# First block in 2 KB rows, wide warm-up matmuls, mask bias by one matmul per bank, first weight part gated one load sooner

## Chip, cores and metric

The kernel runs on one core of one Trainium2 chip. The time is in device microseconds for one launch; lower is better. The median of 9 runs before the change is 224.55 us (223.74 to 226.69).

## The reference, cut to what matters

Sliding-window attention with sinks, for 4 batches of 8 heads, 768 tokens and head size 64, followed by a two-layer feed-forward block on the concatenated heads. A query sees the keys of the last 128 tokens (itself included) and the first 4 tokens of its sequence.

```python
scores = (1 / sqrt(64)) * q @ k.T                      # (4, 8, 768, 768)
keep = (key < 4) | ((0 <= query - key) & (query - key < 128))
a = softmax(where(keep, scores, -1e9))
x = (a @ v).transpose(0, 2, 1, 3).reshape(3072, 512)   # heads side by side
h = x @ w_in                                           # (3072, 2048)
out = (h * sigmoid(1.702 * h)) @ w_out                 # (3072, 512), float32
```

All inputs and the output are float32; the kernel computes in float16 with float32 sums.

## The kernel before, in words

The 3072 tokens are cut into 12 blocks of 256 (`TB`), three to a batch. Each block goes through the same stages: its q, k and v are loaded and cast to float16; q and k are turned so that the head dimension lies on the partitions; scores are computed for four pairs of heads; ACT takes their exponentials; the probabilities are multiplied by v and normalised on DVE; the result x is turned; then x is multiplied by w_in (`mm1`, 64 matmuls of 256 columns), ACT and DVE apply the gate, and the result is multiplied by w_out (`mm2`, 32 matmuls of 512 columns). mm1 of block k stands beside the attention of block k+1, and mm2 of block k beside that of block k+2.

**The order is planned.** Every piece of work is an `Op` with an engine (or several to choose from), an estimated duration, its dependencies, and a due time `prio`. `Plan.run` lays the operations out in time by these estimates, choosing at each step the ready operation that can start first, and by due time among those within 20 ns. It also hands out PSUM banks. Each engine then runs its list strictly in that order on the chip, whatever the real durations are. A change to an estimate, a size or a due time can therefore change the order of work on every engine. Wherever the plan leaves TensorE idle in its first 12 us, `run` puts in filler matmuls on zeros (L142 to L146, `warm` at L883).

**Loads.** `load(k)` issues q, k and v of a block. Block 0 (L409 to L417) comes in eight pieces of 128 KB, four of q on the SyncE queue and four of k on the ACT queue, each with rows of 1 KB; blocks 1 to 3 (L418 to L425) come as two pieces for q and two for k, with rows of 2 KB; later ones in one piece each. q and k of block 1 and v of blocks 0 and 1 are on the SyncE queue, behind q of block 0. The constants, the weights and block 2 are issued by GpSimd (POOL); the weights come in eight parts, w0 to w3 of w_in and w4 to w7 of w_out, cast to float16 by the DMA. A load issued by SyncE or ACT also waits until the one eight before it has landed, since eight semaphores take turns. Some loads are gated by hand (L861 to L879): w0 waits for the last of the four loads of block 1 (`o_first[-1]`).

**Turning and scores of block 0.** The four quarters of block 0 are cast one by one (`o_cqk`), and `turn_two_pairs` turns two pairs of heads of q or k with four TensorE transposes and two copies. So the pairs 0 and 1 can be turned, and their scores computed, when the first half of block 0 is in. Blocks 1 to 3 use `turn_on_pe`, which needs both halves of q (or of k), since each holds every second head; it transposes for every head pair at once, for even or odd token groups. From block 4 on the DMA transposes.

**Mask.** For blocks 0 and 1 the mask is added into the PSUM bank of the scores ahead of them: per bank, three or four matmuls of 128 columns put a bias tile (0 or -60000) there, with the bias as stationary operand and the identity as moving one (L633 to L639). Later blocks multiply the exponentials by a 0/1 mask on DVE (L675).

**Casts.** Casts of blocks 0 and 1 go to DVE, ACT or POOL by the plan's choice; later ones go to POOL. Copies of any kind show as line L282, the helper `copy`; they are told apart by the tiles: qk and v for casts, blkT for copies of turned q and k.

## Time and profile before

| | |
|---|---|
| median of 9 runs | 224.55 us |
| profiled execution: time, span | 223.8 us, 222.0 us |
| TensorE (PE) busy | 215.6 us, 97% of the span |
| DVE / ACT / POOL busy | 127.2 / 125.3 / 86.0 us |
| mm1 matmuls (L775), 768 | 98.7 us, 273 ns each |
| mm2 matmuls (L804), 400 | 99.0 us, 371 ns each |
| filler matmuls (L884), 97 | 7.7 us |
| moved by DMA | 36.42 MB, mean 164 GB/s |

In the rows of the timeline the first number is the start in us from the span's beginning, the second the duration, then engine, line, operation, output and inputs, the count, and in brackets the idle time of the engine before it with what ended the wait. Engine names with a q are the queues that issue transfers, not the transfers. Matmuls overlap, so a row of eight can last a little longer than the distance to the next one; the chain of waits gives those distances. Rows of the windows give, after the stretch and its length, the busy time of PE, PEld, DVE, ACT and POOL with their instruction counts, the granted TensorE clock, the DMA share and the GB/s.

### The profile page before, as it was taken

The page shows a single profiled execution, that of the slowest core. Times are in us where ns is not written, and L with a number is a line of the kernel's source. Part 1 is how long each engine was busy: PE and PEld are TensorE (multiplying, and loading weights), DVE is VectorE, ACT ScalarE, POOL GpSimd, SP SyncE. Part 2 cuts the span into 40 slices and gives each one's busy share as a digit, 9 for nine tenths or more (in the row PEclk, how much of TensorE's full clock was granted, in tenths as well). Part 3 has the DMA queues.
Part 4 walks back from the last instruction along what each step waited for, and adds up shares of the span by engine and source line. Part 5 has one row for each costly group of instructions (what it writes and reads, how often), then busy time and mean ns, then how long its engine had stood idle before and what let it go on. Part 6 is the DMA issues. An engine that isn't in the chain of part 4 may idle for free.

```text
span 222.0 us, 5454 instructions
## 1 busy us (share of the span) xinstructions
PE 215.6 (97%) x2184; PEld 151.1 (68%) x2184; DVE 127.2 (57%) x281; ACT 125.3 (56%) x244; POOL 86.0 (39%) x145
## 2 busy tenths in 40 slices
PE   8989999999999999999999999999999999999993
PEld 8767987467856766766666666767667666666652
DVE  3679766267854865665655664676465655634310
ACT  3676655666747675566476475555476476444320
POOL 3069422665993685801923937507500000000000
PEclk9999999999999999999999999999999999999999
DMA  5999999997948979379399589399442212221223
GB/s 169 301 216 200 191 300 216 326 293 225 270 107 177 274 153 295 76 150 283 94 205 264 78 196 255 69 216 241 93 99 49 64 34 47 52 68 24 50 47 95
DMA packets 66344, 36.42 MB, mean 164 GB/s; under 512 B 28016, under 2 KB 62064, under 8 KB 66320
## 3 DMA queue, kind: packets, MB, share of 16 engines
q1 hardware_dynamic: 60992, 30.06, 54.9%
q0 software_dynamic: 4592, 5.38, 13.1%
q10 hardware_dynamic: 736, 0.66, 1.0%
q8 instruction: 17, 0.28, 0.5%
q14 instruction: 7, 0.06, 0.1%
HBM read 27.43 MB, written 6.29 MB: 152 GB/s over the span
## 4 chain that ended last, share of the span: by engine, by line
PE 88%; DMA 6%; DVE 1%; ACT 1%; SPq 1%; issue 0%; ACTq 0%
PE bank L775 37%; PE bank L804 36%; PE bank L708 7%; PE bank L643 5%; DMA v<-in_v_dram 3%; DMA qk<-in_k_dram 2%; DMA out_dram<-osb 1%; PE bank L747 1%; PE bank L571 1%; PE bank L623 1%; PE bank L636 1%; DVE v L282 1%; ACT at L668 1%; SPq L421 1%; DVE at L675 0%
## 5 line engine op out<-in xcount | busy, mean ns | idle before, releaser
L804 PE MATMUL bank<-w_out,gT 128*128 128x512 f16 (+2 forms) x400 | 99.0, 371 | 0.0
L775 PE MATMUL bank<-xT,w_in 128*128 128x256 f16 x768 | 98.7, 273 | 0.0
L789 DVE SCALAR_TENSOR_TENSOR gT<-th,bank 128x512 f16<-128x512 f16 x96 | 65.5, 683 | 46.7 <-ACT th L787 45.8
L787 ACT ACTIVATE th<-bank 128x512 f16<-128x512 f32 x96 | 57.6, 602 | 57.0 <-PE bank L775 55.5
L775 PEld LDWEIGHTS <-w_in 128*128 128x128 f16 x768 | 73.2, 98 | 23.1 <-issue 1.6
L282 POOL CAST qk<-qk 64x512 f16<-64x512 f32 (+1 forms) x72 | 43.8, 612 | 43.3 <-DMA qk<-in_q_dram 34.9
L668 ACT ACTIVATE at<-bank 128x512 f16<-128x512 f32 (+1 forms) x96 | 48.9, 573 | 15.5 <-PE bank L643 14.3
L804 PEld LDWEIGHTS <-gT 128*128 128x128 f16 x400 | 36.2, 98 | 24.5 <-issue 1.4
L675 DVE TENSOR_TENSOR at<-at,bank 128x1024 f16<-128x1024 f16 (+1 forms) x40 | 25.7, 641 | 23.0 <-ACT at L668 23.0
L282 POOL CAST v<-v 64x512 f16<-64x512 f32 x42 | 26.3, 625 | 9.9 <-DMA v<-in_v_dram 8.0
L708 PE MATMUL bank<-v,at 128*128 128x65 f16 x352 | 21.4, 193 | 0.7 <-DVE v L282 0.5
L823 ACT ACTIVATE osb<-bank 128x512 f32<-128x512 f32 (+1 forms) x24 | 14.5, 602 | 12.4 <-PE bank L804 11.9
L708 PEld LDWEIGHTS <-at 128*128 128x128 f16 x352 | 17.6, 97 | 4.6 <-issue 0.7
L728 DVE TENSOR_TENSOR xb<-bank,rcp 128x256 f16<-128x256 f32 x36 | 15.1, 420 | 0.6
L708 PE MATMUL bank<-vs,ats 128*128 128x65 f16 x128 | 14.9, 193 | 0.0
L708 PEld LDWEIGHTS <-ats 128*128 128x128 f16 x128 | 11.9, 97 | 2.2 <-issue 0.2
L643 PE MATMUL bank<-blkT 64*128 64x256 f16 x192 | 13.5, 244 | 0.0
L643 PEld LDWEIGHTS <-blkT 64*128 64x128 f16 x256 | 8.1, 94 | 6.2 <-issue 3.8
L726 DVE RECIPROCAL rcp<-bank 128x4 f32<-128x4 f32 x48 | 8.5, 177 | 4.9 <-PE bank L708 4.2
L282 ACT COPY blkT<-bank 128x256 f16<-128x256 f16 (+1 forms) x17 | 6.7, 445 | 4.2 <-PE bank L571 2.1
L884 PE MATMUL bank<-zero 128*128 128x128 f16 x97 | 7.7, 244 | 1.0 <-DVE zero L296 1.0
L884 PEld LDWEIGHTS <-zero 128*128 128x128 f16 x97 | 6.9, 112 | 1.1 <-DVE zero L296 1.0
(46 smaller groups left out, 75.5 us busy)
## 6 DMA issues: line engine op xcount, KB each, us to landing
v<-in_v_dram SPq DMA_DIRECT2D x12, 512.0 KB, 7.0
out_dram<-osb SPq DMA_DIRECT2D x46, 128.0 KB, 3.7
qk<-in_q_dram SPq DMA_DIRECT2D x8, 512.0 KB, 4.4
qk<-in_k_dram SPq DMA_DIRECT2D x8, 512.0 KB, 5.8
w_in<-in_moe_w_in_dram POOLq DMA_DIRECT2D x4, 512.0 KB, 7.1
w_out<-in_moe_w_out_dram POOLq DMA_DIRECT2D x4, 512.0 KB, 12.2
qk<-in_q_dram SPq DMA_DIRECT2D x4, 256.0 KB, 5.6
qk<-in_k_dram SPq DMA_DIRECT2D x4, 256.0 KB, 5.7
```

The lines of the kernel that those rows point to most:

```text
L282: {"POOL": nc.gpsimd.tensor_copy, "DVE": nc.vector.tensor_copy, "ACT": nc.scalar.copy}[e](out=out, in_=in_)
L643: nc.tensor.matmul(f32(o_s, 2 * n + i)[:, c : c + w], src[d, j], Q[d].rearrange("d j s -> d (j s)")[:, q0 : q0 + w], start=k >= KM, stop=T ...
L668: nc.scalar.activation(out=A[:, i, 0:W], in_=f32(o_s, 2 * n + i)[:, 0:W], func=AF.Exp, scale=scale)
L675: nc.vector.tensor_tensor(out=A[:, :, 0:W], in0=A[:, :, 0:W], in1=mask[:, c0 : c0 + W].unsqueeze(1).to_broadcast((P, 2, W)), op=ALU.mult,)
L708: nc.tensor.matmul(avp()[:, j, i], a_, v_, start=(n == 0), stop=(n == len(mms) - 1))
L728: o_n = op("DVE", 300, 425, lambda: nc.vector.tensor_tensor(out=X, in0=avp()[:, :, :, 0:D], in1=rc.to_broadcast((P, 2, 2, D)), op=ALU.mult ...
L775: nc.tensor.matmul(f32(holder[0])[:, bass.ts(e, TB)], w_in16[:, c, bass.ts(Fi, P)], X[:, c] if k < KX else X2[:, :, c], start=(c == 0), st ...
L787: o_t = op("ACT", 477, 600, lambda first=first: nc.scalar.activation(out=th[first.places[0]], in_=f32(first), func=AF.Tanh, scale=0.851), ...
L789: o_g[k, s] = op("DVE", 565, 690, lambda first=first, s=s: nc.vector.scalar_tensor_tensor(out=g[:, 2 * s : 2 * s + 2].rearrange("p a t -> ...
L804: nc.tensor.matmul(f32(holder[0])[:, 0:w], g[:, Fi, bass.ts(j, P)], w_out16[:, Fi, c0:c1], start=(Fi == 0), stop=(Fi == NF - 1),)
L823: nc.scalar.mul(O[:, c0:c1], f32(holder[0])[:, 0:w], 0.5)
L884: nc.tensor.matmul(warm_bank[:, 0:P], zero, zero, start=True, stop=True)
```

## The change

- Block 0 is loaded as blocks 1 to 3 are: two pieces each of q and k, 256 KB with rows of 2 KB. It is cast in four pieces of 512 columns and turned with `turn_on_pe` and the permutation that POOL makes (`perm`), with two copies to a transpose group as for block 1. `fours`, `turn_two_pairs` and the second permutation in the constants go.
- The mask bias is laid out transposed and in seven tiles, so that the identity is the stationary operand and one matmul of 384 or 512 columns fills a bank. The constants grow from 520 to 648 columns. DVE makes the seven tiles in two operations, the second for block 1.
- Filler matmuls are 512 columns wide instead of 128, spaced by 400 and later 220 ns in the plan instead of 60. The tile of zeros is four times as wide.
- w0 waits for the last but one load of block 1 (`o_first[-2]`), and the weights may be planned 700 ns sooner. Block 2 (`a2`) and w5 change places in the order of loads.
- The small copy of sink keys for batch 0 (`ks`) gets a due time behind w1, and the indices of hand-gated loads move by four because there are four fewer loads.

```diff
-    turned = np.eye(P).reshape(P, P // 2, 2).transpose(0, 2, 1).reshape(P, P)
-    return np.concatenate([np.eye(P), rel <= 0, rel > 0, turned, sink], axis=1).astype(np.float16)
+    return np.concatenate([np.eye(P), rel <= 0, rel > 0, rel >= 0, rel < 0, sink], axis=1).astype(np.float16)
...
-                while t + 110 < s:
+                while t + 300 < s:
...
-                    t += 60
+                    t += 400 if t < 4500 else 220
...
-    const = pool.tile([P, 4 * P + H], FP16, name="const")
-    ident, perm0 = const[:, 0:P], const[:, 3 * P : 4 * P]
+    const = pool.tile([P, 5 * P + H], FP16, name="const")
+    ident = const[:, 0:P]
...
-    bias = pool.tile([P, 4, P], FP16, name="bias")
+    bias = pool.tile([P, 7, P], FP16, name="bias")
...
-    zero = pool.tile([P, P], FP16, name="zero")
+    zero = pool.tile([P, 512], FP16, name="zero")
...
-    def biases():
-        for n in range(0, 4, 2):
-            nc.vector.tensor_scalar(
-                out=bias[:, n : n + 2].rearrange("p n s -> p (n s)"), in0=const[:, P : 3 * P],
-                scalar1=HIDE, scalar2=-HIDE, op0=ALU.mult, op1=ALU.add,
-            )
-        nc.vector.memset(
-            bias[:, 2:4].rearrange("p n (i a) -> p n i a", i=2)[:, :, :, 0 : n_sink // 2], 0.0
+    def biases(n, x, w):
+        nc.vector.tensor_scalar(
+            out=bias[:, n : n + w].rearrange("p n s -> p (n s)"), in0=const[:, (3 + x) * P : (3 + x + w) * P],
+            scalar1=HIDE, scalar2=-HIDE, op0=ALU.mult, op1=ALU.add,
...
-    o_bias = op("DVE", 400, 500, biases, [o_ident], prio=NEVER + 3, kind="const")
+    def first_biases():
+        biases(0, 0, 2)
+        biases(2, 0, 1)
+        for t in range(2):
+            nc.vector.memset(bias[64 * t : 64 * t + n_sink // 2, 0:2], 0.0)
+    def more_biases():
+        biases(3, 1, 1)
+        biases(4, 0, 2)
+        biases(6, 0, 1)
+    o_bias = [op("DVE", 550, 650, first_biases, [o_ident], prio=NEVER + 3, kind="const"),
+              op("DVE", 500, 600, more_biases, [o_ident], prio=NEVER + 8, kind="const")]
...
-        o_w[j].begin = 9000.0 + 800 * j + (OPT.get('WS',3000) if j > 1 else 0)
+        o_w[j].begin = 8300.0 + 800 * j + (OPT.get('WS',3000) if j > 1 else 0)
...
-    LOADS = OPT.get("LOADS") or ["a0", "a1", "w0", "w1", "w2", "w3", "w4", "w5", "a2", "w6", "w7", "v2"]
+    LOADS = OPT.get("LOADS") or ["a0", "a1", "w0", "w1", "w2", "w3", "w4", "a2", "w5", "w6", "w7", "v2"]
...
-    def fours(c16):
-        return c16.rearrange("s i e h d -> s (i e h d)").rearrange("s (e y i h d) -> s e y i h d", e=2, y=2, i=4, h=2)
...
-            if k == 0:
-                for h in range(4):
-                    def f(e=e, h=h, src=src, dma=dma):
-                        h0 = 4 * (h // 2) + h % 2
-                        return dma.dma_start(
-                            dst[:, e].rearrange("p h i d -> p (h i d)")[:, 256 * h : 256 * h + 256],
-                            src[b, h0 : h0 + 3 : 2, t0 : t0 + TB].rearrange("p (g i) d -> g p (i d)", i=4),
-                        )
-                    lq[e].append(op(eng, 450, (360, 8), f, war, prio=prio + h / 4 + e / 8, kind="load"))
-            elif k < KT:
+            if k < KT:
...
-                    lq[e].append(op(eng, 780 if k == 2 else 450, (850 if k == 3 else 700, 8), f, war, prio=prio + e / 2 + h / 8, kind="load"))
+                    lq[e].append(op(eng, 780 if k == 2 else 450, (850 if k == 3 else 700, 8), f, war, prio=prio + (h / 2 + e / 8 if k == 0 else e / 2 + h / 8), kind="load"))
...
-        elif k == 0:
-            C = fours(c16)
-            for h in range(4):
-                for e in range(2):
-                    def f(eng, e=e, h=h):
-                        copy(eng, C[:, e, h // 2, :, h % 2],
-                             dst[:, e].rearrange("s h i d -> s (h i d)").rearrange("s (h i d) -> s h i d", h=4, i=4)[:, h])
-                    o_cqk[k, e, h] = plan.any(cast(256, CAST_QK[k]), f, [lq[e][h]] + war, prio=NEVER + h, kind="cqk")
...
-                    in1=const[:, 4 * P : 4 * P + H].unsqueeze(2).to_broadcast((P, H, E)), op=ALU.mult,
+                    in1=const[:, 5 * P : 5 * P + H].unsqueeze(2).to_broadcast((P, H, E)), op=ALU.mult,
...
-        if k == 0:
-            for y in range(2):
-                two = [x for e in range(2) for x in turn_two_pairs(e, y, T, fours(c16)[:, e, y])]
-                for p in (2 * y, 2 * y + 1):
-                    o_qkT[k, p] = two
-                o_t.append(two)
-        elif k < KT:
+        if k < KT:
...
-        for p in range(NP) if k else ():
+        for p in range(NP):
...
-            o = op("POOL", 500, 640, ks, o_t + [o_ks0], prio=base - 4 * h8, kind="ks")
+            o = op("POOL", 500, 640, ks, o_t + [o_ks0], prio=base - 4 * h8 if k else load_at("w1") + 4, kind="ks")
+            o.begin = 0.0 if k else 9900.0
...
-    def turn_two_pairs(e, y, T, C):
-        base = attend(0, 0) - 5 * L / 8 + 2 * y + e
-        def tp():
-            for i in range(4):
-                nc.tensor.transpose(f16(o_tp)[:, bass.ts(i, P)], C[:, i].rearrange("s h d -> s (h d)"), perm0)
-        o_tp = op("PE", 4 * pe_ns(P), 3 * pe_ns(P) + P / 2.4 + 166, tp, [o_cqk[0, e, 2 * y], o_cqk[0, e, 2 * y + 1], o_ident],
-                  prio=base, acq=("t", 1), kind="tp")
-        uses("qk16", 0, o_tp)
-        out = []
-        for t in range(2):
-            def f(eng, t=t):
-                copy(eng, T[:, e, 2 * y : 2 * y + 2].rearrange("d p j (t g a) -> d t (p j) g a", t=2, a=2)[:, t],
-                     f16(o_tp).rearrange("d (a t n g) -> d t n g a", a=2, t=2, g=32)[:, t])
-            out.append(plan.any({"DVE": (330, 440), "ACT": (275, 390)}, f, [o_tp], prio=base, kind="cp"))
-        out[1].rel = [(o_tp, 0)]
-        out[1].deps.append(out[0])
-        return out
...
-        parts = [(0, 4), (4, 8)] if k == 1 else [(0, 8)]
+        parts = [(0, 4), (4, 8)] if k <= 1 else [(0, 8)]
...
-                        for c, x in enumerate((1, 0, 1, 0) if r else (2, 3, 0)):
-                            nc.tensor.matmul(
-                                f32(o_s, 2 * n + i)[:, bass.ts(c, P)], bias[:, x], ident, start=c == 0, stop=False,
-                                skip_group_check=True,
-                            )
+                        nc.tensor.matmul(
+                            f32(o_s, 2 * n + i)[:, 0:W], ident, bias[:, 3:7] if r else bias[:, 0:3], start=True, stop=False,
+                            skip_group_check=True,
+                        )
...
-            deps = deps + [o_bias]
+            deps = deps + [o_bias[1 if r else 0]]
...
-            g = o_first[OPT.get("WG", -1)]
+            g = o_first[OPT.get("WG", -2)]
...
-        elif o.kind == "load" and 14 <= n < 27:
+        elif o.kind == "load" and 10 <= n < 23:
...
-        nc.tensor.matmul(warm_bank[:, 0:P], zero, zero, start=True, stop=True)
+        nc.tensor.matmul(warm_bank, zero[:, 0:P], zero, start=True, stop=True)
...
```

## The prediction

> **What bounds the kernel now.** I read the page's first two parts first, then the chain that ended last, then the timeline and the windows of the first 22 us, where the change lies. The page:
>
> ```profile
> PE 215.6 (97%) x2184; PEld 151.1 (68%) x2184; DVE 127.2 (57%) x281; ACT 125.3 (56%) x244; POOL 86.0 (39%) x145
> ...
> PE   8989999999999999999999999999999999999993
> ...
> PEclk9999999999999999999999999999999999999999
> ...
> L884 PE MATMUL bank<-zero 128*128 128x128 f16 x97 | 7.7, 244 | 1.0 <-DVE zero L296 1.0
> ```
>
> TensorE has no free slice between the head and the tail. So a microsecond won or lost before the first matmul with w_in moves the end by a microsecond, and nothing else of this change can. The digits of the head deceive: the 97 matmuls of L884 are filler. What the head truly waits for is in the chain of waits, restricted to 0 to 25 us, and in the timeline:
>
> ```profile
> 1.44 3.94 DMA qk<-in_k_dram
> ...
> 6.62 6.88 DMA v<-in_v_dram
> ...
> 13.98 0.72 DVE v L282
> 14.72 0.44 DVE v L282
> ...
> 17.82 0.61 PE bank L636 x8
> ```
>
> ```profile
> 11.77 0.43 DVE L282 CAST qk<-qk 128x512 f16<-128x512 f32 x1 [0.79 <-DMA qk<-in_k_dram]
> 12.04 1.50 POOL L369 DMA_DIRECT2D w_in<-in_moe_w_in_dram  x2 [1.14 <-DMA qk<-in_k_dram]
> ...
> 13.52 2.14 DVE L282 CAST v<-v 64x512 f16<-64x512 f32 x4 [0.34 <-DMA v<-in_v_dram]
> 13.58 0.61 PE L636 MATMUL bank<-const,bias 128*128 128x128 f16 x8
> ...
> 15.20 0.43 PE L708 MATMUL bank<-v,at 128*128 128x65 f16 x9 [0.47 <-DVE v L282]
> ...
> 17.24 1.56 POOL L369 DMA_DIRECT2D w_in<-in_moe_w_in_dram  x2
> ...
> 17.82 0.61 PE L636 MATMUL bank<-const,bias 128*128 128x128 f16 x8 [0.40 <-DVE xT L754]
> ...
> 21.37 1.04 PE L775 MATMUL bank<-xT,w_in 128*128 128x256 f16 x8
> ```
>
> The last piece of block 1's k lands at 11.7, v of block 0 at 13.5, its casts let probabilities times v run at 15.20, and the first w_in matmul starts at 21.37. Between 15.20 and 21.37 TensorE waits only 0.40. The loads are one saturated stream, as the windows say (last two columns: DMA share, GB/s):
>
> ```profile
> 2.50:6.90 4.40, 4.40 (x71) 4.40 (x70) 1.54 (x8) 2.00 (x4) 0.36 (x2) 1.00 0.93 299
> 6.90:10.60 3.70, 3.45 (x57) 2.75 (x55) 2.51 (x9) 3.14 (x11) 0.20 (x1) 1.00 0.92 301
> 10.60:13.10 2.50, 2.25 (x36) 1.61 (x34) 1.48 (x5) 2.50 (x8) 1.30 (x4) 1.00 1.07 291
> ```
>
> **The change part by part.** The sum is made on the start of the first w_in matmul, 21.37 in the profiled execution (span 222.0, time 223.8); the median of the runs shown is 224.55, 0.75 above, and the difference is added to that median.
>
> 1. *Rows of 2 KB.* Block 0's eight loads of 128 KB become four of 256 KB, the same bytes. The first window above is mostly 1 KB rows, the second mostly 2 KB rows: 299 against 301 GB/s, so no gain. The best three slices of the first 25 us (390, 351 and 318, all in the 2 KB part) would save 1.05 MB x (1/299 - 1/353) = 0.54. I take 0.2, near the windows. The constant grows by one 128-column table, 33 KB, or 0.1. SyncE now issues block 1's loads behind only four others, so they no longer wait for a semaphore of an earlier load (SyncE waited for 0.4 in all there, the last issue was at 5.97, now about 4); the engines were busy anyway. Block 1's last k piece: 11.7 - 0.2 + 0.1 = 11.6.
>
> 2. *What then hangs on that piece.* Before, block 0 was transposed by pairs of heads as quarters landed, and the first score matmul ran at 8.69. Now every transpose needs both halves of q or k (about 7.2), four transposes end at 8.7, and the eight evictions of 0.3 to 0.4 on ACT (5) and DVE (3) give the first scores at about 9.6. That by itself is covered. But the planned order puts all four transposes of block 1 ahead of the scores of pairs 2 and 3 of block 0 on TensorE, and three of these wait for block 1's k. From 11.6: DVE casts (0.43, the row at 11.77), TensorE turns (8 in 0.71, the row at 12.25), and DVE has four evictions of block 1 (0.36 apart, rows of 0.42) where two stood before; it is free at 13.5. The v casts of DVE took 13.52 to 15.16, so they end at 15.1 again, with v landing by 13.5 enough. Probabilities times v resume at 15.2: 0.0. Bounds: -0.5 (all of the 0.54 above) and +0.5 (k no earlier, one cast beside POOL's as slow as the 0.72 in the chain).
>
> 3. *What was done in that wait and is done after it now.* Before, the first score pair of block 1 ran at 13.58 to 14.5, while v was awaited. In the new order the first stands behind the av of pair 1 and the sink scores. All else between 15.2 and the first w_in matmul is alike by count (twelve av groups' parts, six transposes). So TensorE has one more pair there: 0.45 for eight bias matmuls (20.07, in the chain) + 0.33 (row L643 x4 and x2) = **+0.78**. ACT meets block 1's first exponentials later as well (they began at 14.55, now about 16.8, after the last four of block 0), and score banks come free only through ACT. The nearest row is the bank wait at 17.82, 0.40: I take **+0.4**, bounds 0 and 0.8.
>
> 4. *The weight gated one load sooner.* The first w_in issue is behind k's first half (cast at 10.19 without a wait before; about 9.9 now, after POOL's own cast of one q half), not behind its second (12.04). Its first use is at 21.37, and nothing waits for it today, so being sooner gains nothing. It has bytes to take: before, v's stream ended at about 13.8 and the GB/s row fell to 143 and 102 before weights filled it, 2.3 after the issue. Now weights flow from about 12.2, with 0.44 MB of v of block 1 still to move. By the row (one stream of 291 after another) that v lands at its 15.1. [...] w2 is issued behind v's cast on POOL, so not before 17.24 either. Third block and sixth weight part swap places on POOL's queue: a weight part takes 2.56 (0.52 MB at 205), so w5 lands some 2 later, near 34.5, and its first use is near 37: covered.
>
> 5. *Warm-up.* 97 filler matmuls become 16 of 512 columns. They stand in idle time; only the three ahead of the first scores could stand in the way, 3 x 0.216 (L804, 8 in 1.73) = 0.65, while ACT and DVE evict until 9.6: nothing. The larger memset of zero starts them 0.2 later. DVE's bias ops become five and two memsets for two and one: +0.7 (at 0.17 to 0.24 each, from the 0.47 for two), between the constant's landing at 4.2 and a cast that waits for loads until 7.2: nothing, or 0.2 if q's first half is urgent, which it is not.
>
> 6. *Bias matmuls.* Per pair, 8 x 128 columns in 0.45 become 2 x 512 in 2 x 0.216 = 0.43; 6 in 0.335 become 2 x 384 in 0.325. Eight pairs: **-0.1**. The columns, not the count, were the cost.
>
> 7. *Casts of block 0.* Seven of 0.29 on DVE become three of 0.43, -0.7, in time that waits for loads: nothing.
>
> Sum: 0.0 + 0.78 + 0.4 + 0.2 - 0.1 = **+1.3**. The 0.25 that TensorE waits at 70.93 may go or stay; I leave it. 224.55 + 1.3 = 225.85; I say **225.9**.
>
> **Rivals.** *A*, the above: 225.9, own range 224.9 to 227.2. *B, not slower: the loads win.* Place: the last k piece of block 1. If eight loads in flight from the start lift both blocks from 300 to 431 GB/s (the best slice between 13 and 40 us), 2.1 MB x (1/300 - 1/431) = 2.1, and everything through step 3 moves up by it until v (12.2 or so) limits: at most -1.8 against +1.3, giving 224.0. It decides from k landing at about 10.3. For it: slices of 390 exist. Against: the 299 and 301 of whole windows. [...] *E, no effect*: the head's work is merely reordered inside waits that stay, 224.6; it is the lower half of A with steps 3 and 4 at their lower bounds.
>
> **How the numbers follow.** A 0.47, B 0.20, C 0.20, D 0.06, E 0.07. A kernel of this spread tells about 0.5% from no change, 1.1 us: 223.4 and 225.7. Slower: 0.34 of A, all of C and D: 0.60. Same: 0.13 of A, 0.07 of B, E: 0.27. Faster: 0.13 of B, the part where v and k both come at the best rates and the wait at 70.93 goes as well. The range 223.7 to 228.1 leaves out the far half of B's faster part and the far part of C, under 2 in 10.
>
> **What the profile after would show.** Step 1: GB/s of 2.5 to 10.6 (300 now) and DVE's wait for k, near 11.6. Step 2: three transposes of block 1 only after it, four evictions, v casts on DVE until about 15.1. Step 3: the first score pair of block 1 after 15.5 and the first w_in matmul near 22.5. Step 4: w_in issued near 10, v of block 1 cast on DVE near 16.1 with or without a DMA wait. Step 5: PEclk at 9. The prediction is wrong if k lands before 10.3, if v of block 1 lands after 17, or if TensorE is not dense from 18 on.

## The result and the profile after

The changed kernel takes 222.37 us in the median of 17 runs (222.17 to 223.54), the kernel before 224.25 in the median of 54 (223.25 to 226.69). The ratio is 0.9929, with a 95% interval of 0.9912 to 0.9945: 0.7% faster. The forecast was 225.9 and slower, with a range of 223.7 to 228.1, so it was wrong in sign and the time lies below its range.

The 17 times are not one heap. Eleven lie from 222.17 to 222.41 (the earlier group), six from 223.25 to 223.54 (the later one), and nothing between; the granted clock is 0.997 to 1.00 in all of them. The profiled execution, 223.42 with a span of 221.6, is of the later group, and the one of before, 223.80, lies 0.45 under the median of its kernel. Two lines of the page of after, busy time and fillers:

```profile
PE 214.1 (97%) x2063; PEld 143.7 (65%) x2063; DVE 128.6 (58%) x283; ACT 124.9 (56%) x241; POOL 86.2 (39%) x146
...
L844 PE MATMUL bank<-zero 128*128 128x512 f16 x16 | 5.4, 490 | 1.2 <-DVE zero L295 1.2
```

The windows of the same stretches as before (last two columns: DMA share, GB/s). The stream runs at 359 and 341 GB/s where it ran at 299 and 301:

```profile
2.50:6.90 4.40, 3.25 (x16) 1.25 (x15) 1.58 (x10) 1.99 (x3) 0.34 (x1) 1.00 0.98 359
6.90:10.60 3.70, 3.70 (x39) 1.95 (x38) 3.23 (x9) 2.24 (x8) 2.37 (x4) 1.00 1.09 341
10.60:13.10 2.50, 2.50 (x31) 1.36 (x30) 2.18 (x7) 2.50 (x9) 1.04 (x4) 1.00 1.21 259
```

The timeline, for the rows that answer to those of before:

```profile
8.84 1.50 POOL L375 DMA_DIRECT2D w_in<-in_moe_w_in_dram  x2 [0.31 <-DMA qk<-in_k_dram]
...
9.49 1.10 DVE L281 CAST qk<-qk 128x512 f16<-128x512 f32 x2
...
12.21 1.62 DVE L281 CAST v<-v 64x512 f16<-64x512 f32 x3
12.90 0.65 POOL L281 CAST v<-v 64x512 f16<-64x512 f32 x1 [1.14 <-DMA v<-in_v_dram]
13.89 0.43 PE L668 MATMUL bank<-v,at 128*128 128x65 f16 x9 [0.75 <-DVE v L281]
...
15.77 1.06 POOL L479 TENSOR_TENSOR vs<-vs,const 128x520 f16<-128x520 f32 x1 [2.22 <-DMA vs<-in_v_dram]
15.91 1.20 DVE L281 CAST v<-v 64x512 f16<-64x512 f32 x1
...
17.36 0.38 PE L596 MATMUL bank<-bias,const 128*128 128x512 f16 x1 [0.74 <-DVE xT L714]
...
21.63 1.03 PE L735 MATMUL bank<-xT,w_in 128*128 128x256 f16 x8
```

The last loads of block 1 are cast from 9.49, the very last at 9.82 (11.77 before), av (the probabilities times v) resumes at 13.89 (15.20), and yet the first w_in matmul comes at 21.63 (21.37). The chain of waits of 0 to 25 us tells what heads it now: not q, k or v, but the landing of the constants, and later a cast of 1.20 us, nearly three times its usual 0.42. The first cast on VectorE stands behind the bias operations until 6.61, though the first q and k are there at 4.05 and 4.72:

```profile
1.23 3.95 DMA const<-const
...
5.20 0.43 DVE bias L317 x2
...
6.43 0.14 DVE seen L305
6.57 0.05 issue
6.61 0.09 DVE qk L281
...
15.91 1.20 DVE v L281
17.11 0.21 DVE xT L714
17.32 0.04 issue
17.36 0.38 PE bank L596
```

After the first w_in matmul the kernel before had one stall left, the "0.25 at 70.93" of the prediction; in the chain of before it looks so, and in the chain after TensorE goes through this place without a wait:

```profile
67.83 0.47 issue
68.30 0.59 ACT at L668
...
70.93 0.51 PE bank L708 x11
```

It helps to split each profiled time into the start of the first w_in matmul and all the rest. Before: 223.80 = 21.37 + 202.43. After, later group: 223.42 = 21.63 + 201.79. The rest is 0.64 shorter, the head 0.26 longer. Of the 0.64, 0.36 lie before VectorE's last operation (218.25 before, 218.15 after, so 196.88 and 196.52 behind the first w_in matmul): that is the stall. The other 0.28 come behind it, and they belong to that one profile of before: e2 and e12 below have the stall, but end as after does (5.26 and 5.25 behind that operation, against 5.55 before and 5.27 after). The earlier group (profile in e9, the changed kernel once more): 222.66 = 20.88 + 201.78.

### The profile page after: what moved, and what is told of

Its sections match the earlier page's. It is cut to its first block, busy times and chain, and to the rows that moved or that the text cites. A ratio compares the mean times of both kernels' runs of the same rounds, so it can differ in the third digit from the quotient of the medians.

```text
span 221.6 us, 5201 instructions
## 1 busy us (share of the span) xinstructions
PE 214.1 (97%) x2063; PEld 143.7 (65%) x2063; DVE 128.6 (58%) x283; ACT 124.9 (56%) x241; POOL 86.2 (39%) x146
## 4 chain that ended last, share of the span: by engine, by line
PE 92%; DMA 3%; DVE 3%; issue 1%; ACT 0%; SPq 0%; DVEq 0%; POOLq 0%
PE bank L735 38%; PE bank L764 36%; PE bank L668 7%; PE bank L603 5%; DMA const<-const 2%; PE bank L532 1%; DVE v L281 1%; PE bank L596 1%; DMA out_dram<-osb 1%; PE bank L707 1%; PE bank L584 1%; DVE blkT L281 1%; PE bank L844 0%; DVE bias L317 0%; ACT osb L783 0%
## 5 line engine op out<-in xcount | busy, mean ns | idle before, releaser
L281 POOL CAST qk<-qk 64x512 f16<-64x512 f32 (+1 forms) x73 | 44.4, 611 | 43.3 <-DMA qk<-in_q_dram 37.4
L281 POOL CAST v<-v 64x512 f16<-64x512 f32 x42 | 25.8, 615 | 12.8 <-DMA v<-in_v_dram 10.8
L281 ACT COPY blkT<-bank 128x256 f16<-128x256 f16 (+1 forms) x14 | 5.4, 473 | 7.4 <-PE bank L532 7.3
L603 PE MATMUL bank<-blkT,blkT 64*128 64x128 f16 x64 | 7.2, 222 | 0.0
L844 PE MATMUL bank<-zero 128*128 128x512 f16 x16 | 5.4, 490 | 1.2 <-DVE zero L295 1.2
```

Of the source, the lines that this page charges most:

```text
L281: {"POOL": nc.gpsimd.tensor_copy, "DVE": nc.vector.tensor_copy, "ACT": nc.scalar.copy}[e](out=out, in_=in_)
L603: nc.tensor.matmul(f32(o_s, 2 * n + i)[:, c : c + w], src[d, j], Q[d].rearrange("d j s -> d (j s)")[:, q0 : q0 + w], start=k >= KM, stop=T ...
```

## The experiments

**What made the loads faster.** Row length, or the number of loads? *e1*: the changed kernel with block 0 in eight loads of 64 partitions, rows of 2 KB kept.

```diff
+            if k == 0:
+                for h in range(4):
+                    def f(e=e, h=h, src=src, dma=dma):
+                        y, z = h // 2, slice(64 * (h % 2), 64 * (h % 2) + 64)
...
+                            dst[z, e].rearrange("p h i d -> p (h i d)")[:, 512 * y : 512 * y + 512],
+                            src[b, y::2, t0 + P * (h % 2) : t0 + P * (h % 2) + P].rearrange("p (g i) d -> g p (i d)", i=8),
```

> The changed kernel, but block 0 again in eight loads of 128 KB, each of 64 partitions with rows of 2 KB. So the rows are those of the change, and the number of loads and SyncE's waits for earlier loads are those of before. Theory R (the length of the rows sets the rate): 2.5 to 6.9 us stays near 350 GB/s (359 after, 299 before), time near 222.4. Theory F (fewer loads, so that block 1's are issued without waiting, set the rate): it falls to about 300 GB/s, block 1's last k is cast 1.5 us later, and the time is 223.5 to 224.5.

*e2*: the kernel before with block 0 in four loads of 256 KB, rows of 1 KB kept.

```diff
-                for h in range(4):
+                for y in range(2):
...
-                            src[b, h0 : h0 + 3 : 2, t0 : t0 + TB].rearrange("p (g i) d -> g p (i d)", i=4),
+                            src[b, 4 * y : 4 * y + 4, t0 : t0 + TB].rearrange("(p x) (g i) d -> g p x (i d)", x=2, i=4),
```

> The kernel before, but block 0 in four loads of 256 KB that still have rows of 1 KB; turning, order of block 0's work, bias and warm-up as before. Theory R: 2.5 to 6.9 us stays near 300 GB/s and nothing is won, 224.2 or, since a quarter now waits for its half, up to 0.5 more. Theory F: 340 to 360 GB/s there, block 1's last k at about 10 instead of 11.7, and 1 us or more is won, about 223.

e1 took 223.71 (223.53 to 223.93; ratio 0.9960, 0.9941 to 0.9980), e2 223.14 (222.88 to 223.38; 0.9945, 0.9926 to 0.9964). Their windows, e1 and then e2:

```profile
2.50:6.90 4.40, 3.48 (x14) 1.35 (x12) 1.30 (x8) 2.11 (x3) 0.35 (x1) 1.00 1.03 258
6.90:10.60 3.70, 2.58 (x26) 1.62 (x27) 2.30 (x8) 1.16 (x5) 0.61 (x1) 1.00 1.05 334
```

```profile
2.50:6.90 4.40, 4.40 (x51) 4.40 (x50) 1.47 (x9) 1.58 (x3) 0.34 (x1) 1.00 0.99 330
6.90:10.60 3.70, 3.70 (x65) 3.23 (x62) 1.43 (x5) 2.93 (x10) 0.00 (x0) 1.00 1.09 346
```

With 2 KB rows in eight loads the first stretch is slow (258), with 1 KB rows in four loads it is faster (330). From before over e2 to after it goes up by about 30 GB/s with fewer loads and again with longer rows (299, 330, 359), the second stretch only with fewer loads (301, 346, 341; e1 has 334 there), and the last k of block 1 lands at 11.74 before, at 9.53 in e2 and at 9.29 in after: of the 2.45, 2.21 came with fewer loads. e1's loads also span only 64 partitions each, and before has 299 with eight loads too, so e1's 258 is not the count alone.

With fewer loads ahead of them, and without the wait for an earlier landing (0.4 in before), block 1's loads are also issued sooner. SyncE's row in before, e1, e2 and after:

```profile
5.39 1.19 SPq L421 DMA_DIRECT2D qk<-in_k_dram  x2
```

```profile
5.96 1.26 SPq L424 DMA_DIRECT2D qk<-in_k_dram  x2
```

```profile
3.79 1.25 SPq L420 DMA_DIRECT2D qk<-in_k_dram  x2
```

```profile
3.40 1.25 SPq L415 DMA_DIRECT2D qk<-in_k_dram  x2
```

Whether the earlier issue or the size of a load made the stream faster isn't separated: no run holds the issue back. The landing of the constants shows a price: they come by GpSimd's queue beside these loads, and landed at 4.2 (before, 130 KB) and 4.8 (e1, 162 KB) with eight loads, and at 5.3 to 5.6 (e2, e12, 130 KB) or 5.1 to 5.9 (162 KB) with four.

*e3*: the kernel before with the change's loads, casts and turning of block 0 (and the table of constants that goes with them); its fillers, bias, gate and order of loads are those of before.

```diff
-            if k == 0:
-                for h in range(4):
...
-            elif k < KT:
+            if k < KT:
```

> The kernel before with the first part of the change alone: block 0 in one piece of 2 KB rows for each half of q and k, cast and turned like block 1; narrow warm-up, narrow bias matmuls, gate and order of loads as before. If the load is what wins, this has all of the gain, 222.4, or more than that since DVE has fewer bias operations ahead of its first cast. If the other three parts win too, it stays at 223 or above.

224.36 (223.82 to 224.85; 1.0010, 0.9985 to 1.0034): no gain by itself. Its windows show 358 and 343 GB/s, and av resumes at 14.28 instead of 15.20. But from there to the first w_in matmul it takes 7.33 instead of 6.17, and the 0.9 won is given back. Part of that is step 3's extra score pair; the profile has the lost meeting described below as well.

**The other parts, undone one at a time in the changed kernel.** *e5* brings back the narrow fillers, *e6* the old bias, *e7* the old gate, *e8* the old order of loads:

```diff
-                    t += 400 if t < 4500 else 220
+                    t += 60
...
-                            f32(o_s, 2 * n + i)[:, 0:W], ident, bias[:, 3:7] if r else bias[:, 0:3], start=True, stop=False,
+                        for c, x in enumerate((1, 0, 1, 0) if r else (2, 3, 0)):
...
-            g = o_first[OPT.get("WG", -2)]
+            g = o_first[OPT.get("WG", -1)]
...
-    LOADS = OPT.get("LOADS") or ["a0", "a1", "w0", "w1", "w2", "w3", "w4", "a2", "w5", "w6", "w7", "v2"]
+    LOADS = OPT.get("LOADS") or ["a0", "a1", "w0", "w1", "w2", "w3", "w4", "w5", "a2", "w6", "w7", "v2"]
```

> The changed kernel with the narrow filler matmuls of before (128 columns, spaced by 60 ns in the plan). Theory L (loads win, the rest is small): 222.4 within 0.3. Rival P (the other three parts hold the 2 us between the load alone, 224.4, and the whole change, 222.4): if it is the filler, 223 or more, because some 60 fillers in a row with their weight loads end later than eleven wide ones and hold up TensorE's first real work (after the masks).

> The changed kernel with three or four bias matmuls of 128 columns per bank and the two bias operations of DVE as before. Theory L: 222.4 within 0.3; by columns eight pairs cost 0.1 more on TensorE, and DVE has 0.7 less to do between the constants' landing and its first cast, which could win up to 0.5. Rival P: 223 or more if the bias holds the 2 us.

> The changed kernel with w0 gated by the last load of block 1 again, and planned 700 ns later. Theory L: 222.4 within 0.3. [...] Rival P: 223 or more if the first weights, issued at 8.8 after the change and at 9.7 where the load alone was changed, hold the 2 us.

> The changed kernel with w5 ahead of block 2 in the order of loads again. Theory L: 222.4 within 0.3 up to 0.4 more, since the wait of 0.47 and 0.25 that TensorE has near 68 to 71 us before, and not after, may come back with this order. Rival P: 223 or more if the order holds the 2 us.

Medians: e5 223.91 (ratio 0.9971, 0.9946 to 0.9997), e6 223.56 (0.9952, 0.9930 to 0.9974), e7 223.59 (0.9973, 0.9947 to 0.9998), e8 224.36 (0.9995, 0.9970 to 1.0019). They mix the two groups in different shares, so the profiles say more:

| | constants landed | first w_in matmul | rest |
|---|---|---|---|
| after | 5.20 | 21.63 | 201.79 |
| e5, old fillers | 5.74 | 22.22 | 201.78 |
| e6, old bias | 5.78 | 22.89 | 201.68 |
| e7, old gate | 5.72 | 22.05 | 201.82 |
| e8, old order | 5.58 | 21.92 | 202.45 |

The gate leaves both the rest and the distance from the landing (16.43, 16.33) where they were: it is worth nothing that shows. So do the fillers at first sight (16.48), but not on the way: the first cast of v on VectorE starts 7.31 after the landing in e5 and 7.01 in after, since more filler time lies in the chain (1.34 against 1.08 between the mask and the scores), and the 0.3 disappears in a wait of VectorE that is described below (a cast of 0.88 in e5, 1.20 in after). Where that wait is absent, narrow fillers should cost 0.3; e5's two fastest times, 223.04 and 223.05, are 0.6 above the earlier group, and a later landing of the constants would have to account for the remainder.

The old order of loads costs 0.66 in the rest; and e8's only early time, 223.16, is 0.9 above e7's, 222.28. e6 has its first w_in matmul 0.7 later by its distance from the landing, but not by the bias matmuls: its 16 transposes took 1.61 in the chain where after's took 1.03, and four fillers took 1.71 where two took 0.43, so up to 10.8 TensorE ran slower, the fillers at half their pace. What the bias part is worth for the whole is left open by this run.

*e12* adds the new order to e2 (its text says block 1 where the edit is on block 0):

> The kernel before with block 1 in four loads of 256 KB (rows of 1 KB, its old way of turning; 223.14 as e2) and now also the new order of loads, third block ahead of the sixth weight part. If the order takes 0.6 off the time after the first w_in matmul whatever the head does, 222.5, with 201.8 from that matmul to the end. The rival, that the order helps only together with the new casts and score order, expects 223.1.

223.37 (222.86 to 223.65; 0.9959, 0.9943 to 0.9975), no better than e2's 223.14; the rest is 202.13 in e12 and 202.14 in e2, and the stall at 67 to 71 is still there. So the order alone doesn't take the stall away. The distance from the first w_in matmul to VectorE's last operation sorts the kernels: 196.88 in before, e2 and e12 (block 0 turned as before, either order), 197.01 in e3 and 197.16 in e8 (new turning, old order), 196.50 to 196.53 in after, e5, e9, e13 and e16 (both new). e8 loses its 0.64 in another place than before does, between 53 and 56. There matmuls with w_in stand right behind the transposes of x and wait for VectorE's copy of x (53.24 to 53.53), and the pieces up to 56.3 are stretched too; after has four matmuls with w_out in between. The chain in e8, then in after:

```profile
52.49 0.44 PE bank L603 x8
...
53.59 1.14 PE bank L735 x9
```

```profile
52.58 0.44 PE bank L603 x8
...
53.29 0.86 PE bank L764 x4
54.16 0.87 PE bank L735 x8
```

The list of waits doesn't show this, since each of the pieces is under a tenth of a microsecond there; the starts of the matmuls do (0.33 apart at 53.26 in e8, where 0.11 is usual). New turning with the old order swaps one loss for another, and only both together have neither.

**Are the constants the new bound?** *e4* has SyncE load them first; *e9* is the changed kernel again, as a control; *e10* puts the bias operations and the mask behind the first casts; *e11* doubles the constants' width with columns that nobody reads.

```diff
-    o_ident = op("POOL", 700, (300, 8), lambda: nc.gpsimd.dma_start(const, const_d.ap()), prio=NEVER - 1, kind="load")
+    o_ident = op("SP", 450, (300, 8), lambda: nc.sync.dma_start(const, const_d.ap()), prio=NEVER - 1, kind="load")
```

```diff
+    o_bias[0].begin, o_bias[1].begin = 7000.0, 8800.0
+    o_seen.begin = 12500.0
```

```diff
-    const = pool.tile([P, 5 * P + H], FP16, name="const")
+    const = pool.tile([P, 10 * P + H], FP16, name="const")
```

> The changed kernel with the constants loaded from SyncE's queue ahead of q instead of from POOL's. After the change the constants land at 5.17 us, DVE waits for them from 1.8 to 5.2 and then makes the bias before its first cast, and the chain that ended last begins with them. Theory K (the constants' landing is now what the head waits for): they land near 4, DVE's casts come 0.7 to 1 us sooner, and the time falls to 221.4 to 222.0. Rival: v of block 0 or DVE's own work bounds the head right behind, and it stays within 0.3 of 222.4.

> The changed kernel once more, with nothing edited, as the control for the three others. Expected 222.2 to 223.4. The theory that the landing of the constants sets the head says: start of the first w_in matmul = landing of the constants (start of the first bias operation) + 16.4, and time = that start + 201.8, whatever the landing is in this profile; if the constants land at 4.1 to 4.5 the time is 222.3 to 222.7, if at 5.2 to 5.7 it is 223.4 to 223.9. The rival, that the landing only happened to be late in the profiles so far and block 1's loads set the head, expects the first w_in matmul at the same time within 0.2 whatever the landing.

> The changed kernel with the bias operations and the mask after the first casts of q and k in the order of VectorE, so that these casts don't stand behind the constants. If the constants set the head, the first q and k casts start about 5.5 to 6.0 instead of 6.6, and the first w_in matmul comes 0.5 to 1.2 sooner: 221.5 to 222.2 in all. The order also puts the first score pair of block 1 ahead of the first attention-times-v matmuls as it was in the kernel before, so that part of a gain may come from there (step 3 of the prediction: 0.8 at most). The rival, that the loads of block 1 set the head, expects no change from the casts: 222.4 to 223.4, less whatever the score pair gives.

> The changed kernel with a constant of twice the width (five more identity blocks that nobody reads; nothing else is changed), so that the constants land later. If they set the head, a landing that is later by 0.3 to 1.0 makes the first w_in matmul and the whole time later by as much: 222.8 to 224. The rival, that block 1's loads set the head, expects 222.4 to 222.8: only the 164 KB more that the queues carry.

e4: 222.88 (222.02 to 224.55; 0.9939, 0.9910 to 0.9969). The constants were there at 3.08, but then the first cast on VectorE waited for q until 6.42, TensorE stood 2.0 before the mask, and the clock that was granted fell to 0.58 (third last column of the second row; the profiled execution, 224.55, is its slowest):

```profile
2.50:6.90 4.40, 2.67 (x12) 1.06 (x10) 1.64 (x9) 1.07 (x2) 0.34 (x1) 1.00 0.93 309
6.90:10.60 3.70, 3.36 (x23) 2.26 (x24) 2.49 (x9) 1.40 (x5) 1.10 (x2) 0.58 1.01 329
```

e11: 224.32 (223.81 to 225.30; 1.0004, 0.9979 to 1.0029), landing at 6.38 and the first w_in matmul at 22.67: 1.18 later lands, 1.04 later starts, against after. The constants do set the head when they land so late (both profiles have the lost cast described next). e9: 223.05 (222.43 to 223.67; 0.9949, 0.9927 to 0.9971), four times in each group. Its profile refuted half of my expectation: the constants landed at 5.63, *later* than after's 5.20, and yet the first w_in matmul came at 20.88, 0.75 *sooner*. So the landing is one term, and something else makes the groups. e10: 222.64 (222.37 to 222.75; 0.9920, 0.9891 to 0.9949), one group, first casts at 5.20.

**What makes the two groups.** In e9's timeline VectorE's second cast of block 1's v (15.91 in after; the expectations below call it the third, counting GpSimd's) runs before GpSimd's multiplication of the sink values (L479), not just behind its start:

```profile
12.64 1.31 DVE L281 CAST v<-v 64x512 f16<-64x512 f32 x3
...
13.53 0.89 POOL L281 CAST v<-v 64x512 f16<-64x512 f32 x1 [1.07 <-DMA v<-in_v_dram]
...
16.03 0.42 DVE L281 CAST v<-v 64x512 f16<-64x512 f32 x1
...
16.46 1.06 POOL L479 TENSOR_TENSOR vs<-vs,const 128x520 f16<-128x520 f32 x1 [2.04 <-DMA vs<-in_v_dram]
```

In after the multiplication runs from 15.77 to 16.83 and the cast ends at 17.11, 0.28 behind it. In the profiles of before, e3, e5, e7, e8, e10, e11 and e16, too, a cast that overlaps it ends 0.28 to 0.30 after it. The kernel before loses this meeting as well:

```profile
16.23 1.06 POOL L493 TENSOR_TENSOR vs<-vs,const 128x520 f16<-128x520 f32 x1
...
16.59 0.99 DVE L282 CAST v<-v 64x512 f16<-64x512 f32 x1
```

In these rows the multiplication keeps its 1.06, as in e9, where the cast is done before it, and the cast is pushed behind it. But the cast ends 0.28 behind it and takes 0.42 alone, so either 0.14 of the two overlap or the end of GpSimd's record is late by that much. What the two engines contend for, no run shows.

The same thing happens 3 us sooner. In after GpSimd's cast of 12.90 goes first and VectorE's third cast of block 0's v takes 0.75; in e9 VectorE goes first with 0.44, and GpSimd's cast takes 0.89. By losing there VectorE comes to the second meeting at 15.91, behind 15.77; 0.31 sooner, by what the first meeting cost, it would have been ahead.

*e13* cuts the multiplication to one head of eight, with the order of every engine kept, and leaves the sink values of the other seven at zero; *e14* loads the sink values sooner and multiplies them ahead of GpSimd's v cast; *e15* is e14 with e10's late bias; *e16* is the control.

```diff
+                H2 = H if b else 1
...
-                    out=vs16[:, b].rearrange("r p i e -> r (p i) e"), in0=vs32[:, b].unsqueeze(1).to_broadcast((P, H, E)),
+                    out=vs16[:, b].rearrange("r p i e -> r (p i) e")[:, 0:H2], in0=vs32[:, b].unsqueeze(1).to_broadcast((P, H2, E)),
```

```diff
-            return nc.sync.dma_start(
+            return nc.gpsimd.dma_start(
...
-            o_vs[b].begin = max(0.0, nominal(k - 2, 0))
+            o_vs[b].begin = nominal(k - 2, 0) if k else 10300.0
```

> The changed kernel with GpSimd's multiplication of the sink values (L479, 1.06 us beside the third cast of v in the second part) cut to an eighth, one head instead of eight; every engine keeps its order. It leaves out seven eighths of the sink values of the first batch (they stay zero). If the two groups of times (222.2 to 222.7 and 223.3 to 223.7) come from VectorE's cast having to wait for that multiplication, the second group is gone: every time within 222.0 to 222.7, median 222.3, and the cast takes 0.42 instead of 1.20. The rival, that the groups come from the landing of the constants, keeps both groups, 222.2 to 223.7.

> The changed kernel with the four small loads of the sink values issued by GpSimd at the start instead of by SyncE after v, and the multiplication placed before GpSimd's cast of v (about 10.5 to 11.6 by the rows of the profile after), so that it is over before VectorE casts v. Nothing is left out. If waiting for GpSimd makes the second group: 222.0 to 222.7 without a second group, less what the later cast of v on GpSimd (about 0.8 later) gives back. The rival, the constants: both groups stay.

> Both: the sink values early as in e14, and the bias operations after the first casts as in e10, where the cast always waited for GpSimd (16.23 to 17.53). If each gain is its own, e10's 222.64 less the 0.8 of that wait: 221.6 to 222.0, under both kernels. If the loads of block 1 bind by then (second piece of q landed at 7.0 in e10): 222.2 to 222.6.

> The changed kernel unedited, as the control for the three before it. Expected in two groups, 222.2 to 222.7 and 223.3 to 223.7. Where the profiled execution falls in the second, VectorE's third cast of v ends 0.28 after GpSimd's multiplication ends; where it falls in the first, the cast is done, in 0.42, before the multiplication begins.

e16: 222.27 (222.16 to 223.62; 0.9939, 0.9919 to 0.9960), eight times from 222.16 to 222.33 and four from 223.32 to 223.62; the profiled one is of the later group, with L479 from 15.66 to 16.72 and the cast until 17.00. e13: 222.44 (222.10 to 222.81; 0.9929, 0.9906 to 0.9952), and no later group. Its timeline:

```profile
15.56 0.43 DVE L281 CAST v<-v 64x512 f16<-64x512 f32 x1
...
15.69 0.45 POOL L480 TENSOR_TENSOR vs<-vs,const 128x65 f16<-128x65 f32 x1 [1.74 <-DMA vs<-in_v_dram]
```

Its constants landed at 5.15 and the first w_in matmul started at 20.41. With after (5.20, 21.63) that parts the landing from the meetings: the same landing, and 1.22 between the two. But e13 also won the first meeting, so it doesn't price the second alone; and with 14 of the 37 times of the changed kernel in the later group, six without one would come by chance about once in 17 (an estimate from these counts).

e14 was slower than the changed kernel, 223.61 (223.27 to 223.88; 0.9983, 0.9969 to 0.9996), in one group: the multiplication now ran at 12.08 to 13.14, right where VectorE begins to cast v, and behind it GpSimd's cast and the issues of the next weights (13.84 to 16.1). Five v casts in a row took 3.43 us there. e15: 224.49 (223.97 to 224.80; 1.0011, 0.9993 to 1.0029); its chain also runs over a copy, the gate and the exponentials of later blocks from 34.8 to 38.7. Moving the sink values moved the collision, it didn't remove it.

*e17* keeps the changed kernel and every order in it, and adds one wait: L479 waits for the cast of 15.91. *e18* does the same to e10, where the last cast of that v took 1.28 in the profile (16.23 to 17.51); its line names `o_cv[1, 0][3]`.

```diff
+    gates.append((o_vs[0], o_cv[1, 0][2]))
     for o, g in gates:
```

> The changed kernel with one wait added and nothing else: GpSimd's multiplication of the sink values waits for VectorE's third cast of v (second part), so that it can never begin just ahead of it; the order on every engine is that of the changed kernel. If the lost race makes the second group: no second group, 222.2 to 222.7 in all runs, with the cast at 0.42 us and the multiplication right behind it. The rival, that a multiplication 0.3 to 0.7 us later is itself on the path (the sink matmuls need it, and the third and fourth weight parts are issued behind it): 222.8 to 223.4 in all runs.

> The kernel with the bias operations after the first casts (e10, 222.64) and the same wait: the multiplication behind the cast that took 1.28 us at 16.23 there, each engine's order as in e10. If that cast's wait was on the path: 0.8 less than e10, 221.7 to 222.1, under the changed kernel's first group. The rival, that block 1's loads or the later multiplication bind instead: 222.4 to 222.8, as e10.

e17: 223.09 in one group of 0.22 (223.03 to 223.25; 0.9949, 0.9930 to 0.9968). e18: **221.98** (221.72 to 222.29; 0.9902, 0.9880 to 0.9923), the lowest median of all kernels here; the changed kernel has no time under 222.16 in any of its 37 runs. Against the kernel before the intervals of the two ratios overlap (0.9912 to 0.9945 for the changed kernel), so the lead is small. Timelines of e17 and then e18, and e18's chain:

```profile
16.48 0.43 DVE L281 CAST v<-v 64x512 f16<-64x512 f32 x1
...
17.04 1.06 POOL L479 TENSOR_TENSOR vs<-vs,const 128x520 f16<-128x520 f32 x1 [2.93 <-DVE v L281]
```

```profile
16.04 0.43 DVE L281 CAST v<-v 64x512 f16<-64x512 f32 x1
...
16.61 1.05 POOL L481 TENSOR_TENSOR vs<-vs,const 128x520 f16<-128x520 f32 x1 [2.27 <-DVE v L281]
```

```profile
1.19 6.10 PE bank L846 x16
7.29 0.46 PE bank L534 x8
...
20.27 0.87 PE bank L737 x8
```

e18's chain begins with fillers: constants and loads are no longer at its head.

The profiles in which VectorE and GpSimd keep the changed kernel's order give the sum (without e5, whose v casts start 0.3 later). All starts are counted from the landing of the constants; the first meeting is that of VectorE's third cast of block 0's v with GpSimd's cast, the second that of VectorE's next but one cast with L479:

| | GpSimd's cast begins | VectorE's third cast begins, takes | cast at the second meeting begins, takes | first w_in matmul |
|---|---|---|---|---|
| after | 7.70 | 7.89, 0.74 | 10.71, 1.20 | 16.43 |
| e16 | 7.76 | 7.90, 0.75 | 10.73, 1.07 | 16.32 |
| e7 | 7.68 | 7.99, 0.74 | 10.81, 1.00 | 16.33 |
| e8 | 7.83 | 7.90, 0.82 | 10.80, 1.01 | 16.34 |
| e11 | 7.69 | 7.90, 0.74 | 10.71, 1.06 | 16.29 |
| e17 | 7.80 | 7.91, 0.79 | 10.78, 0.43 | 15.74 |
| e9 | 7.90 | 7.90, 0.43 | 10.40, 0.42 | 15.25 |
| e13 | 7.90 | 7.90, 0.43 | 10.41, 0.43 | 15.26 |

The first meeting decides the second. Where it is lost, VectorE comes at 10.7 or later, behind the multiplication (10.43 to 10.57 in the first five rows); where it is won, at 10.40, ahead of it. And the first is decided by two landings: GpSimd's cast starts 0.05 after block 1's v lands, VectorE's third cast 7.9 after the constants, and a difference of a tenth parts the groups. That the runs without a profile split for the same reason is inferred.

The second meeting costs 0.55 to 0.75 (e17 against the five above it). The first costs about 0.4: e17's other 0.1 against e9 comes from a third meeting, that of the next cast (17.85, 0.53 instead of 0.43) with the multiplication that now runs until 18.10. e17 has one group, but not the early one: in its profile it lost the first meeting, and its constants landed 0.5 later than after's, which is why the expectation of 222.2 to 222.7 was missed. The added wait can't help with the first meeting.

## Why the prediction was wrong

By its own steps, with a profile in which both meetings are won (e13, head 20.41, which stands in for the earlier group although it leaves out sink values) set against before (21.37), and then the later group.

- *Step 1 failed.* "299 against 301 GB/s, so no gain", 0.2 taken, k at 11.6. The window of mostly 1 KB rows and that of mostly 2 KB rows ran alike, and I read that as a rate that loads can't change. It compared row lengths; what the change altered was how many loads the same bytes come in. That block 1's loads would be issued sooner was seen, and put at nothing because "the engines were busy anyway". Measured: 359 and 341 GB/s, and block 1's last k landed at 9.29 instead of 11.74, 2.45 sooner. Rival B had the place, the direction and the point from which it decides (k landed before 10.3), at 0.20.
- *Step 2* took its 0.0 from step 1. av resumed at 13.53 (e13) or 13.89 (after) instead of 15.20: -1.67 or -1.31.
- *Step 3 was about right in its first term.* +0.78 was forecast for the score pair that is done after the wait; from av to the first w_in matmul it takes 6.88 in e13 and 6.87 in e9 against 6.17: +0.71. Before has a wait of 0.40 in there, the lost second meeting, and e13 waits for 0.16 in all, so the added work itself is about 0.95 (an estimate from these numbers). The +0.4 for a bank wait isn't there. In the later group 7.74, and the 0.74 that TensorE waits at 17.36 is the lost second meeting: a wait in the place I named, but with another cause.
- *Step 4*: no run shows the sum's +0.2, a delay of v of block 1 by the weights (C, at 0.20, is a longer one). In after that v lands at 12.85, 1.76 behind that of block 0 (1.72 before), its casts from 15.0 wait for no transfer, and e7, with the old gate, has 1.73. In e2, e3 and e12 it lands 3.1 to 3.2 behind; that the weights did it there isn't shown, since e7 issues its weights at about the time of e3 (10.10 and 9.73).
- *Step 5 failed in its cover.* The bias operations lie "between the constant's landing at 4.2 and a cast that waits for loads until 7.2: nothing". But the cover was made of two loads, and the change moved both: q came sooner, the constants a microsecond later (+0.1 was allowed). Now the casts wait behind them (6.61), and the head moves with the landing, 0.47 for 0.48 between e9 and e13. Taking the bias out of the way (e10) without the collision (e18) gives 20.11, 0.3 under e13. The wide fillers were put at nothing; by e5 they save about 0.3 where no other wait covers it.
- *Step 6*: -0.1. The rows agree (0.34 and 0.45 for the matmuls of a pair in e6's chain once it ran at full pace, 0.33 and 0.43 in after); what it is worth in the end isn't measured.
- *The order of loads* was called covered, and "the 0.25 at 70.93 may go or stay; I leave it". It went: 0.36 of the rest, with the new turning and the new order together, so it wasn't true that nothing behind the first w_in matmul could gain. With the new turning and the old order as much or more was lost in another place (197.01 in e3, 197.16 in e8, against 196.88). I looked at what w5 being later might cost, and not at what block 2 being sooner changes in the order on TensorE.

The sum with what was measured: -1.67 (steps 1 and 2) + 0.71 (step 3) - 0.36 (the stall) = -1.3, and -0.28 by the end of before's profile, which isn't the change's: 223.80 - 1.6 = 222.2, e13's own time, and the earlier group's (222.17 to 222.41). The later group loses 1.2 of it again. The medians lie 1.9 apart, and before's profile 0.45 under its median. A lower clock in the head, D with its 0.06, didn't come in the changed kernel: in after TensorE waited 1.14 before the mask, and the granted clock was 1.00 in all three windows. In e4, where it waited 2.0 there, the granted clock was 0.58 from 6.9 to 10.6; that the wait brought this isn't shown.

## What to carry to other kernels

A bandwidth read from a window is that of the loads as they were cut (here 299 GB/s with eight, 330 and 359 with four): before taking it for a limit, ask whether the change alters their number, and what else is loaded beside them: here block 1's last k landed 2.45 sooner, and the constants, 33 KB larger, 0.97 later. When a cost is called hidden, write down both ends of its cover and move them by the change's own effects first. When times of one kernel fall in two groups, compare a profile of each and look for a pair of instructions that swap places; one added wait can fix their order. It ended the two groups in e17, but moved the median the wrong way, as an earlier meeting was still lost and the wait brought on a later one; e18, with the path ahead of it shortened too, gained. So follow such a chain of meetings back to its first.

## What the runs showed of the hardware that was not expected

- From 2.5 to 6.9 us, with four loads of 256 KB for block 0 the stream ran at 330 (1 KB rows) to 359 GB/s (2 KB rows), with eight of 128 KB at 299 (before) and 258 (e1). With four the constants, on GpSimd's queue, landed 0.3 to 1.4 us later.
- In the profiles of before, after, e3, e5 to e8, e10 to e12 and e14 to e17 a VectorE cast from float32, 0.42 alone, that started while GpSimd multiplied ended 0.28 to 0.30 after the multiplication, whether it had begun 0.18 (e14) or 1.00 (e10) before that end; in after VectorE came 0.14 us late (15.91 against 15.77), and its cast took 1.20. A copy out of PSUM wasn't held up: xT took 0.26 at 17.11 in e17, in the middle of the multiplication, and 0.25 at 17.32 in after, behind it.
- In e14 VectorE's casts took 0.66 to 0.74 while GpSimd was issuing weight loads; in e13 one at 16.93 took its usual 0.43 there. What makes the difference is open.
- In e6 TensorE ran slower up to 10.8, though the granted clock was 1.00 there: four fillers took 1.71 and 16 transposes 1.61, against 0.43 for two and 1.03 in after. It had begun with ten fillers of 512 columns at about 0.44 each, and a pause of 0.62 came before the mask's last matmuls.
